# Two small reads of the weight matrices ahead of their rows, and an x tile on another queue

## The chip, the cores and the metric

The kernel runs on one core of one Trainium2 chip. The time is that of one execution on the device in microseconds (us), and the median of three runs of the kernel before is 178.54 us (178.52 to 178.56). The core has a matrix engine (TensorE, PE in the profile, with its weight loads as PEld), a vector engine (VectorE, DVE), an engine for functions of single elements (ScalarE, ACT), GpSimd (POOL) and SyncE (SP), which issues transfers here. 16 DMA engines move the data, whoever issues the transfer.

## The reference, cut to what matters

x has 2048 rows (tokens) of 512 elements, in bf16. The layer norm of x feeds two branches, and both are added to x: a linear recurrence over time with 512 complex states (branch A), and a gated feed-forward network with 1376 hidden columns (branch B).

```python
xn = _layernorm(x, axis=-1)
# branch A: h[t] = Lam_bar * h[t-1] + xn[t] @ B_bar ; y = 2 Re(h C^T) + xn * Dskip
# branch B:
g = _silu(xn @ w_gate)          # w_gate: 512 x 1376
u = xn @ w_up                   # w_up:   512 x 1376
y = (g * u) @ w_down            # w_down: 1376 x 512
out = x + A(xn) + B(xn)
```

## The kernel before

**Tiling.** The 2048 tokens are 16 tiles of 128 (`xall[:, n, :]`), and four tiles are a chunk of 512. The 512 input columns are four blocks of 128 (`KD = 4`, index k), which is the depth over which each matmul sums. The gate and up matrices come in as rows: row k is the block of 128 matrix rows with the first 1024 of the 1376 columns (`wu01`, `wg01`, 256 KB each, `load_row`, L117); the other 352 columns of all four blocks come as one transfer for each matrix into `w_end` (L113).

**The start.** TensorE first runs nine matmuls on a constant (L675). Tokens 0 to 255 (x tiles 0 and 1) take a way of their own, so that work can begin before the layer norm is known: VectorE sums each row of x (L222), TensorE transposes the tile (L231, `raw_mm`) and spreads the negative mean (L243, `mean_mm`), ScalarE copies the transposed tile out (L240, `raw_copy`), and VectorE adds the mean to it (L248, `centered`; six pieces, in the order tile 0 block 0, tile 0 block 1, tile 1 block 0, tile 1 block 1, then the last two blocks of tile 0 and of tile 1). Then TensorE multiplies these tokens by up row 0, 1, 2, 3 (L494, `row_mm(0, k)`: two tiles by two column groups, four matmuls for each row), and after that by gate row 0 to 3, with the transposed parameters (L278) and tile 2 (L231) in between. The factor 1/sigma of the layer norm comes in later, when ScalarE copies the sums out (L514, L502). VectorE meanwhile forms the statistics (L182, L183), GpSimd the inverse root (L192), and VectorE the normalised tiles (L200).

**What follows.** SyncE transposes the four normalised tiles by DMA (L258) and then the two parts of the matrix B (`BT`, L145). TensorE does the rest of chunk 0's gate and up (L494, L774), and then for each chunk the projection by B (L387, `bproj_tile`), gate and up (L462, L548), and the output by the down weights (L605) and by the matrix C folded with the parameters (L618, with `CF` from L373). VectorE carries the recurrence (L429) with its rotations (L397 to L411). Its operations are put between TensorE's by a fixed plan of costs (`pump`), at build time; each engine then works through its own list in order.

**Queues.** SyncE issues, in this order: x tile 0 (L123), up rows 0 to 3, gate rows 0 and 1, x tile 2 (L131), gate row 2, x tile 3 (L133), gate row 3, the two ends of the weights, x tiles 4 to 7 (L141), the transposes of x (L258), those of B (L145). ScalarE's queue carries x tile 1 (L125) behind a memset of VectorE (L124) that writes two elements of that tile, so that the transfer waits for it; then ScalarE loads its table of functions (L126). GpSimd's queue carries three parameter rows of 1 KB (L140).

The transfers of SyncE and ScalarE tell of their landing by eight semaphores that are handed out in turn, and a transfer is issued only when the one that had its semaphore before has landed. So x tile 2 waits for x tile 0, gate row 2 for x tile 1, x tile 3 for up row 0, gate row 3 for up row 1, the two ends for up rows 2 and 3, and x tiles 4 to 7 for gate row 0.

Of the kernel before, what the change touches and what calls it, by code (L numbers as in the profile page):

```python
# [11 lines left out]
BF16 = mybir.dt.bfloat16  # L12
# [11 lines left out]
def kernel(  # L24
# [17 lines left out]
    nc = tc.nc  # L42
# [21 lines left out]
    const = ctx.enter_context(tc.tile_pool(name="const", bufs=1))  # L64
# [15 lines left out]
    x_v = A_x[0].rearrange("(n p) d -> p n d", p=128)  # L80
# [5 lines left out]
    xall = const.tile([128, NT, D], BF16, name="xall")  # L86
# [33 lines left out]
    ident = const.tile([128, 128], BF16, name="ident")  # L120
    make_identity(nc, ident[:])
    minus_mean = const.tile([128, 128], BF16, name="minus_mean")
    nc.sync.dma_start(out=xall[:, 0, :], in_=x_v[:, 0, :])  # L123
    nc.vector.memset(xall[:, 1, 0:2], 0.0)  # L124
    nc.scalar.dma_start(out=xall[:, 1, :], in_=x_v[:, 1, :])  # L125
    nc.scalar.preload_act_table_set("silu_and_others")  # L126
    for k in range(KD):
        load_row(nc.sync, wu01, wu_v, k)
# [779 lines left out]
```

## Time and profile before

| | us |
|---|---|
| median of three runs | 178.54 |
| the profiled execution | 178.45 |
| its span, from the first to the last instruction | 176.2 |
| TensorE busy | 171.9 |
| VectorE busy | 157.6 |
| ScalarE busy | 102.7 |
| GpSimd busy | 28.1 |

The span is what the profile covers; the time of the execution has some work around it. Each line of a timeline gives the start in us, the time that it covers, engine, line of the program, operation, what is written from what, shape and count, and in brackets how long the engine was idle before it and what ended that. A queue's own instructions, which issue transfers, have a q behind the engine's name. For the transfers the profile gives the size and the time from issue to landing. In a table by stretches each engine has its busy time and the number of its instructions, and behind them stand the clock that TensorE was granted (1.00 is full), the mean busy share of the 16 DMA engines and what they moved in GB/s.

### The profile page before, as it was taken

Reading aid. Unit: us, or ns where it says so; the run is one execution under the profiler, and the core shown is the slowest. Engines: PE = TensorE matmul, PEld = TensorE weight load, DVE = VectorE, ACT = ScalarE, POOL = GpSimd, SP = SyncE. Lnnn points to the kernel's source line nnn. Section 1 sums busy time; section 2 is a strip of 40 time slices with the busy share of each in tenths; the row PEclk is TensorE's granted clock in tenths of the full one; section 3 lists DMA queues with packets and bytes.
Section 4 is the critical chain, followed back from the end, with each engine's and each line's share of the span. In section 5 each row is a group of like instructions: output and inputs, shape, how many; then the busy total and the mean of one; then the engine's idle time right before and its main releaser. Section 6 shows DMA issues by size and latency. Waiting matters only on the chain.

```text
span 176.2 us, 2377 instructions
## 1 busy us (share of the span) xinstructions
PE 171.9 (98%) x859; PEld 81.9 (46%) x859; DVE 157.6 (89%) x261; ACT 102.7 (58%) x188; POOL 28.1 (16%) x39
## 2 busy tenths in 40 slices
PE   7899999999999999999999999999999999999993
PEld 4344445464444444446444444446444444444543
DVE  3877999999999999999999999999999998699542
ACT  4179599794996685236598661024666653991100
POOL 5244110022000000044300000024100000521700
PEclk9999999999999999999999999999999999999999
DMA  5997949999999300037016000007310000696831
GB/s 169 357 342 147 142 90 208 287 188 297 151 221 309 119 0 4 0 34 85 2 30 123 0 0 0 0 0 80 43 20 12 0 0 4 93 159 106 91 87 60
DMA packets 34042, 17.87 MB, mean 101 GB/s; under 512 B 24896, under 2 KB 32928, under 8 KB 33984
## 3 DMA queue, kind: packets, MB, share of 16 engines
q1 hardware_dynamic: 30288, 14.22, 34.5%
q0 software_dynamic: 3456, 3.28, 14.6%
q10 hardware_dynamic: 288, 0.23, 0.4%
q8 instruction: 6, 0.10, 0.2%
q14 instruction: 4, 0.03, 0.1%
HBM read 8.03 MB, written 5.24 MB: 75 GB/s over the span
## 4 chain that ended last, share of the span: by engine, by line
PE 95%; DMA 3%; SPq 0%; DVE 0%; issue 0%
PE ps L462 29%; PE ps L605 22%; PE ps L618 16%; PE ps L387 16%; PE ps L494 7%; PE ps L548 3%; DMA wu<-in_B_w_up_dram 3%; PE ps L774 2%; SPq L117 0%; SPq L123 0%; DVE xall L621 0%; PE ps L231 0%; PE ps L278 0%
## 5 line engine op out<-in xcount | busy, mean ns | idle before, releaser
L605 PE MATMUL ps<-wd_sb,guT 128*128 128x512 bf16 (+4 forms) x187 | 38.9, 366 | 0.0
L429 DVE TENSOR_TENSOR_SCAN g<-r_t,car,u 128x512 bf16<-128x512 f32 x24 | 29.1, 1265 | 0.0
L618 PE MATMUL ps<-CF,wt 128*128 128x512 bf16 (+2 forms) x136 | 28.5, 366 | 0.0
L387 PE MATMUL ps<-xnT,BT 128*128 128x512 bf16 x128 | 28.3, 379 | 0.0
L605 PEld LDWEIGHTS <-guT 128*128 128x128 bf16 (+1 forms) x187 | 17.9, 98 | 20.5
L462 PE MATMUL ps<-xnT,wu 128*128 128x512 bf16 x96 | 24.6, 379 | 0.0
L462 PE MATMUL ps<-xnT,wg 128*128 128x512 bf16 x96 | 24.6, 379 | 0.0
L625 POOL DMA_DIRECT2D out_dram<-res x12 | 10.5, 1043 | 78.5 <-ACT res L624 72.5
L476 ACT ACTIVATE guT<-ps 128x512 bf16<-128x512 f32 x30 | 18.2, 606 | 4.9 <-PE ps L462 4.5
L477 ACT CAST u<-ps 128x512 bf16<-128x512 f32 x30 | 17.9, 595 | 4.8 <-PE ps L462 4.7
L389 ACT CAST u<-ps 128x512 bf16<-128x512 f32 x32 | 17.6, 594 | 4.9 <-PE ps L387 3.6
L618 PEld LDWEIGHTS <-wt 128*128 128x128 bf16 x136 | 13.0, 98 | 14.7
L387 PEld LDWEIGHTS <-BT 128*128 128x128 bf16 x128 | 12.5, 98 | 14.9
L624 ACT CAST res<-ps 128x512 bf16<-128x512 f32 x12 | 6.8, 585 | 21.4 <-PE ps L618 21.4
L579 ACT ACTIVATE xr<-xall,nb,rstd 128x512 bf16<-128x512 bf16 x16 | 11.8, 807 | 8.7 <-DVE xall L587 4.7
L462 PEld LDWEIGHTS <-wu 128*128 128x128 bf16 x96 | 9.4, 98 | 11.3
L462 PEld LDWEIGHTS <-wg 128*128 128x128 bf16 x96 | 9.3, 98 | 10.6
L192 POOL TENSOR_TENSOR rstd<-ve,neg_half 128x1 f32<-128x1 f32 (+1 forms) x7 | 7.5, 1077 | 29.4 <-DVE ve L191 28.9
L182 DVE BATCH_NORM_STATS2 stats<-xall 128x6 f32<-128x512 bf16 x16 | 10.8, 676 | 0.2 <-DMA xall<-in_A_x_dram 0.2
L462 PE MATMUL ps<-xnT,w_end 128*128 128x512 bf16 x48 | 10.8, 379 | 0.0
L481 DVE TENSOR_TENSOR guT<-guT,u 128x1024 bf16<-128x1024 bf16 x15 | 10.1, 676 | 0.0
L397 DVE TENSOR_TENSOR pm<-g,c 128x2048 bf16<-128x2048 bf16 x8 | 9.8, 1222 | 0.1
(121 smaller groups left out, 207.5 us busy)
## 6 DMA issues: line engine op xcount, KB each, us to landing
out_dram<-in_A_x_dram SPq DMA_DIRECT2D x3, 512.0 KB, 5.3
out_dram<-res POOLq DMA_DIRECT2D x12, 128.0 KB, 3.2
out_dram<-xall POOLq DMA_DIRECT2D x3, 512.0 KB, 6.7
wd_sb<-in_B_w_down_dram SPq DMA_DIRECT2D x1, 1280.0 KB, 7.9
wu<-in_B_w_up_dram SPq DMA_DIRECT2D x4, 256.0 KB, 4.6
wg<-in_B_w_gate_dram SPq DMA_DIRECT2D x4, 256.0 KB, 5.1
xall<-in_A_x_dram SPq DMA_DIRECT2D x1, 1024.0 KB, 6.9
xall<-in_A_x_dram SPq DMA_DIRECT2D x1, 512.0 KB, 6.2
```

The costliest lines, as they stand in the source:

```text
L182: nc.vector.bn_stats(out=stats[:, n, 0, :], in_=xall[:, n, :])
L387: nc.tensor.matmul(ps[:] if c else by_k(ps[:]), lhsT=BT[:, part, k, q * 128:(q + 1) * 128], rhs=xnT[:, c, k, :] if c else xnT0[:, k], star ...
L389: nc.scalar.copy(out=u_tiles[c][:, part, q, :], in_=ps[:])
L429: V.tensor_tensor_scan(out=g()[:, part, q, :], data0=r_t[:, q:q + 1].to_broadcast([128, CW]), data1=u_tiles[c][:, part, q, :], initial=ini ...
L462: nc.tensor.matmul(ps[:fs, lo:hi], lhsT=wslice(groups, fi, k), rhs=xnT[:, c, k, lo:hi], start=(k == 0), stop=(k == KD - 1))
L476: nc.scalar.activation(out=guT[:fs, fi, :], in_=psg[:fs], func=ACT.Silu)
L477: nc.scalar.copy(out=u_pair[c][:fs, fi % 2, :], in_=psu[:fs])
L494: nc.tensor.matmul(ps[:, 0:(b - a) * 128], lhsT=tokens(i, k), rhs=groups[gi][:, k, 0:(b - a) * 128], start=(k == 0), stop=(k == KD - 1))
L579: nc.scalar.activation(out=box["xr"][:], in_=xall[:, n, :], func=ACT.Identity, scale=rstd[:, n:n + 1], bias=nb[:, n:n + 1])
L605: nc.tensor.matmul(o[:], lhsT=gu_tiles[c][:fsz[fi], fi, i * 128:(i + 1) * 128], rhs=wd_sb[:fsz[fi], fi, lo:hi], start=(fi == 0), stop=False)
L618: nc.tensor.matmul(o[:], lhsT=w_tiles[c][:, part, q, i * 128:(i + 1) * 128], rhs=CF[:, part, q, lo:hi], start=False, stop=(part == 1 and q ...
L625: nc.gpsimd.dma_start(out=out_v[:, n, lo:hi], in_=res[:, lo:hi], accum_op=ALU.add)
```

## The change

A new tile `early` takes two elements (4 bytes) of each of 32 matrix rows, every 16th one, of the up matrix and then of the gate matrix. Nothing reads it. The two transfers are the first on ScalarE's queue. x tile 1 goes to SyncE's queue, between x tile 0 and the up rows, and the memset is left out.

```diff
+    early = const.tile([32, 2, 2], BF16, name="early")
     nc.sync.dma_start(out=xall[:, 0, :], in_=x_v[:, 0, :])
-    nc.vector.memset(xall[:, 1, 0:2], 0.0)
-    nc.scalar.dma_start(out=xall[:, 1, :], in_=x_v[:, 1, :])
+    for i, v in enumerate((B_w_up, B_w_gate)):
+        nc.scalar.dma_start(out=early[:, i, :], in_=v.rearrange("(r s) f -> r s f", r=32)[:, 0, 0:2])
+    nc.sync.dma_start(out=xall[:, 1, :], in_=x_v[:, 1, :])
     nc.scalar.preload_act_table_set("silu_and_others")
     for k in range(KD):
         load_row(nc.sync, wu01, wu_v, k)
```

A matrix row has 2752 bytes, so the touched places lie 44,032 bytes apart. With one transfer more ahead of the rows, the semaphores move by two places: gate row 0 is issued when x tile 0 has landed, gate row 1 after the early read of up, x tile 2 after the early read of gate, gate row 2 after x tile 1; x tile 3 waits for up row 0, gate row 3 for up row 1, and the others as before. No other instruction is added, removed or put in another order on any engine.

## The prediction

> **What bounds the kernel now.** I read the chain of waits first, then the first 23 us engine by engine, because the chain says that nothing after them matters by itself.
>
> ```profile
> span 176.2 us, 2377 instructions
> PE 95%; DMA 3%; SPq 0%; DVE 0%; issue 0%
> 1.65 4.53 DMA wu<-in_B_w_up_dram
> 6.18 0.04 issue
> 6.22 3.61 PE ps L494 x16
> ```
>
> The profiled execution took 178.45 us for a span of 176.2, so 2.25 lie around the span; the median of the runs shown is 178.54, 0.09 above it. TensorE is the chain from 6.22 on, back to back to the end. What stands ahead of it is one transfer: the second row of the up weights, issued at 1.65 and landed at 6.18. So the time can fall only if TensorE begins its unbroken run earlier, and only as far as nothing later makes it wait. The timeline of TensorE and VectorE shows the start closely:
>
> ```profile
> 3.13 0.42 DVE L222 SCALAR_TENSOR_TENSOR xnT<-xall 128x256 bf16<-128x256 bf16 x1 [1.59 <-DMA xall<-in_A_x_dram]
> 3.50 0.43 DVE L222 SCALAR_TENSOR_TENSOR xnT<-xall 128x256 bf16<-128x256 bf16 x1
> 4.01 1.67 DVE L248 TENSOR_TENSOR CF<-xnT,ps 128x128 bf16<-128x128 bf16 x6
> 4.88 0.33 PEld L494 LDWEIGHTS <-CF 128*128 128x128 bf16 x3 [0.41 <-DVE CF L248]
> 6.22 2.75 PE L494 MATMUL ps<-wu,CF 128*128 128x512 bf16 x12 [0.73 <-DMA wu<-in_B_w_up_dram]
> 8.81 0.38 PE L494 MATMUL ps<-wg,CF 128*128 128x512 bf16 x1
> ```
>
> The twelve matmuls of rows 1 to 3 run from 6.22 to 8.81, 0.216 each. Their tokens were ready long before: six centering pieces in 1.67 from 4.01 are 0.28 each, so the four that row 1 needs were there at 4.01 + 4 x 0.28 = 5.13. Row 0's last two matmuls began at 4.88 and gave way at 4.88 + 2 x 0.216 = 5.31. Without the wait for row 1, TensorE goes on at 5.31 instead of 6.22: 0.91 us are there to be had.
>
> Why row 1 is late is in the transfers, grouped by stretches (columns: PE, PEld, DVE, ACT, POOL busy, granted clock, DMA share, GB/s), and in the issues with size and time to landing:
>
> ```profile
> 3.50:4.50 1.00, 0.89 (x10) 0.59 (x8) 0.93 (x6) 0.92 (x4) 0.04 (x1) 1.00 0.85 261
> 4.50:5.50 1.00, 0.99 (x4) 0.21 (x3) 0.96 (x4) 0.28 (x2) 0.00 (x0) 1.00 0.93 298
> 6.50:7.50 1.00, 1.00 (x6) 0.42 (x5) 0.93 (x4) 0.00 (x0) 0.58 (x1) 1.00 1.03 374
> 7.50:8.50 1.00, 1.00 (x6) 0.49 (x5) 0.51 (x4) 0.07 (x1) 0.66 (x1) 1.00 1.05 391
> 39.50:41.00 1.50, 1.50 (x9) 0.69 (x7) 1.43 (x5) 1.11 (x4) 1.35 (x2) 1.00 0.91 185
> 42.50:44.00 1.50, 1.50 (x9) 0.69 (x7) 1.50 (x4) 0.19 (x1) 0.00 (x0) 1.00 1.08 371
> wu<-in_B_w_up_dram SPq DMA_DIRECT2D x1, 256.0 KB, 2.9
> ```
>
> From 3.5 to 5.5, when up rows are read for the first time, the engines of the DMA are 0.89 busy and move 280 GB/s, which is 314 for a full share; from 6.5 to 8.5 they move 382 at 1.04, 368 for a full share. Busy but moving less means packets that stand still. The first touch of the down weights shows it again: 185 / 0.91 = 203 for a full share in its first 1.5 us, 371 / 1.08 = 344 three microseconds later. A transfer is landed when its slowest engine is done, so a few stalled packets cost row 1 far more than the mean. Row 0 landed at 1.19 + 2.9 = 4.09; at 368 GB/s the next 256 KB need 0.71, so row 1 would be there at about 4.8 without stalls, ahead of 5.31.
>
> **The change part by part.** *Gone:* the memset of VectorE and ScalarE's wait for it, 0.06 us ahead of an engine that waits for x until 3.13 anyway: nothing. *Moved:* x tile 1.
>
> ```profile
> 0.74 0.39 SPq L123 DMA_DIRECT2D xall<-in_A_x_dram  x1
> 0.90 0.37 ACTq L125 DMA_DIRECT2D xall<-in_A_x_dram  x1
> 1.19 1.84 SPq L117 DMA_DIRECT2D wu<-in_B_w_up_dram  x4
> 1.31 1.28 ACT L126 ACT_TABLE_LOAD   x1 [1.31 <-DVE e_t L162]
> 3.58 1.20 ACT L240 CAST xnT<-ps 128x256 bf16<-128x256 f32 x4 [0.99 <-PE ps L231]
> xall<-in_A_x_dram SPq DMA_DIRECT2D x1, 128.0 KB, 2.4
> xall<-in_A_x_dram ACTq DMA_DIRECT2D x1, 128.0 KB, 2.5
> prm_rows<-in_A_Lambda_re_dram POOLq DMA_DIRECT2D x1, 1.0 KB, 4.0
> ```
>
> Its issue goes from 0.90 on ScalarE to 1.19 on SyncE, and every row behind it is issued 0.43 later (0.74 to 1.19 is one issue). Landing: at best as fast as tile 0, 1.19 + 2.4 = 3.6; at worst like the transfer that stands second on that queue now, 1.19 + 2.9 = 4.1. Its sum started at 3.50, when VectorE came free, so the centering chain slips by 0.1 to 0.6; I take 0.2, nearer to tile 0, which has the same size. The later issue of the rows costs nothing: row 1 is issued at 1.65 and the DMA comes to it only after row 0, landed at 4.09; 0.43 lies inside that queue time. If the queue were empty, it would be the whole 0.43.
>
> *Added:* two issues on ScalarE ahead of the table load. At 0.37 to 0.43 each from 0.74 on, the load starts at 1.6 and ends at 2.9; ScalarE's first copy is at 3.58, so it is covered with 0.7 to spare. New waits stand on SyncE's queue, since landing semaphores are handed out in turn: the first gate row waits for x tile 0, the second for the early up transfer, x tile 2 for the early gate transfer, the next for x tile 1. SyncE comes to them at about 3.5, 3.9 and 4.4. An early transfer lands like x tile 1 (0.74 + 2.5 = 3.2) or, if it meets stalls, like the 1 KB parameter row (4.0 after issue: 4.7 to 5.2). Gate rows and everything behind on that queue would be held up to 0.8 then, with rows 1 to 3 of up still to be moved: covered.
>
> *What the touches do to the DMA:* the trace has no row for a 4-byte read. Bounds for the delay of x and thereby of the chain: 0, if the touches run beside tile 0, when the engines are not full; and 1.4, row 1's own lateness (6.18 - 4.8), which is that of the slowest engine. Between them stands the first touch of the down weights, 203 instead of 344 for a full share over 1.5 us, 0.41 x 1.5 = 0.6 us lost per engine on average. I take 0.1, near the lower end, because the touches come while the DMA has little else to do. With the 0.2 above the centering chain slips by s = 0.3.
>
> Here a rule speaks against the change. The 1 KB parameter row needed 4.0 us where 128 KB of x needed 2.5: a small transfer lands with the stalls of its neighbours. The Trainium skill, "DMA: Bandwidth & Descriptors", section "Queues, rings and completion order", says that an engine's semaphore increment lands only after every earlier write of that engine, across its queues; by that rule a stalled touch holds back x although x stands on another queue. The parameter row agrees; whether touches stall, no row shows. By it s would be at its upper end and the time that of the second rival.
>
> *What takes over.* If row 1 comes in time, TensorE gains 0.91 - s. The next thing it waits for is the transposed B matrix:
>
> ```profile
> 8.48 0.41 DVE L200 TENSOR_SCALAR CF<-xall,mv,rstd 128x512 bf16<-128x512 bf16 x1 [0.46 <-POOL rstd L192]
> 9.14 0.69 DVE L182 BATCH_NORM_STATS2 stats<-xall 128x6 f32<-128x512 bf16 x1 [0.24 <-DMA xall<-in_A_x_dram]
> 12.17 0.73 DVE L200 TENSOR_SCALAR CF<-xall,mv,rstd 128x512 bf16<-128x512 bf16 x2 [0.59 <-POOL rstd L192]
> 12.61 2.69 SPq L258 DMA_TRANSPOSE xnT<-CF  x2
> 15.35 3.92 SPq L145 DMA_TRANSPOSE BT<-in_A_B_re_dram  x1
> BT<-in_A_B_re_dram SPq DMA_TRANSPOSE x1, 6.8
> 22.69 6.79 PEld L387 LDWEIGHTS <-BT 128*128 128x128 bf16 x32
> 67.34 5.38 DVE L373 SCALAR_TENSOR_TENSOR CF<-CT,nc2im,cm 128x512 bf16<-128x512 bf16 x8
> 73.04 5.13 PE L618 MATMUL ps<-CF,wt 128*128 128x512 bf16 x23
> ```
>
> B lands at 15.35 + 6.8 = 22.15 and is loaded at 22.69: 0.54 to spare. Its issue follows, on SyncE, the transposes of x, which follow VectorE's normalising at 12.17, and that chain goes back through 9.14 and 8.48 to the centering. In it stands one wait for a transfer, 0.24 for x tile 2, which goes if the slow engines are no longer late; then B moves by s - 0.24. So B allows TensorE to be early by 0.54 + 0.24 - s = 0.78 - s. That is below 0.91 - s and decides. Further on, the four C pieces that the first output needs are ready at 67.34 + 7 x 0.67 = 72.0 for matmuls up to 73.04 + 3 x 0.216 = 73.7: 1.6 to spare, no bound.
>
> The sum: 178.45 - (0.78 - 0.3) = 177.97 for an execution like the profiled one, and 0.09 more for the median: 178.06, rounded to **178.1**.
>
> **The rivals.** *The stalls stay.* They may belong to each DMA engine by itself, or to something else at that time, such as the parameter transfers of GpSimd. For it: the gate rows, first touched after 6.5, run at 368 without a slow start, so first touch alone isn't the rule. Against it: the slow start of the down weights. Then row 1 lands at 6.18 as before, or up to 0.43 later by the issue: 178.54 to 178.97, likeliest 178.6. x late by 0.3 would not show, since tokens are ready 0.9 ahead.
>
> *The stalls move in front of x (slower).* The touches stall on the same 16 engines, ahead of x tile 1 and of the rows; place: VectorE's second sum at 3.50, and all that follows to B. Price: s. From s = 0.78 on the kernel is slower than before; with the touches at 1.0 (midway between 0.6 and 1.4) and 0.2 of x tile 1's move s is 1.2 and the time 178.54 + 1.2 - 0.78 = 178.96; at both upper ends, 1.4 + 0.6, it is 179.76. For it: 64 touches on 16 engines are four each, one behind the other, and the lateness of the parameter row. Against it: the first quarter of up rows landed in 2.9 in spite of first touch.
>
> *Half way:* the stalls go, but s lies between 0.42 and 0.78, and the gain is under 0.36: 178.2 to 178.55.
>
> **How the numbers follow.** 0.2% of 178.54 is 0.36 us, about what a measurement of this kernel can tell from no change; so the bounds are 178.18 and 178.90. Forecast 0.47 (177.75 to 178.18, from s = 0 to 0.42); half way 0.10; stalls stay 0.20, of which 0.15 within the bounds and 0.05 above; stalls in front of x 0.23. Faster 0.47, within 0.25, slower 0.28. The range for 8 of 10 goes from the lower end, s = 0, 177.76 rounded to 177.7, up to 179.1, into the slower rival; the forecast's own is 177.75 to 178.2.
>
> **What would show it.** Right: the idle time of TensorE ahead of row 1's matmuls is below 0.2, the DMA's rate for a full share from 3.5 to 5.5 is near 368, the matmuls of the gate start at about 8.2 instead of 8.81, and a short wait for B stands at about 22.2. x tile 1's sum starts at 3.7. Wrong: row 1 is still awaited after 6.1 (the stalls stayed), or the second sum starts after 4.3 (they moved in front of x). A gain above 0.8 would mean that B isn't bound to VectorE's chain.

## The result and the profile after

| | before | after |
|---|---|---|
| median of 22 executions each, taken together (us) | 178.51 | 178.94 |
| their range | 178.1 to 179.29 | 178.44 to 181.0 |
| the profiled execution | 178.45 | 180.63 |
| its span | 176.2 | 178.6 |
| first matmul of the gate | 8.81 | 10.87 |
| from the end of the last matmul to the end of the span | 2.71 | 3.08 |

The kernel became slower: ratio 1.0043, interval 1.0024 to 1.0062. The mean rose by 0.77, more than the median, because the executions spread: six of the 22 took 179.98 to 181.0 (mean 180.51), the other sixteen have a mean of 178.80, which is 0.30 above the mean of before, 178.50. The profiled execution is one of the six. One of them, 180.54, has a span of only 177.0; its excess lies outside the span, as with one execution of before (179.7 with a span of 176.4). So two things are to be explained, 0.3 us in most executions, and nearly 2 us in about a quarter of them.

The page's head and the shares of the chain after:

```profile
span 178.6 us, 2377 instructions
PE 95%; DMA 1%; DVE 1%; SPq 0%; issue 0%; DVEq 0%
```

The chain of waits after (start, duration, what):

```profile
1.19 2.36 DMA xall<-in_A_x_dram
...
4.47 0.83 DVE CF L250 x3
5.32 6.58 PE ps L496 x20
```

TensorE is again the chain to the end, and the transfer ahead of it is shorter. But the work takes longer in it: 20 matmuls in 6.58, where before's chain had 16 in 3.61 and four more add 0.86. The timeline after:

```profile
0.74 0.41 ACTq L126 DMA_DIRECT2D early<-in_B_w_up_dram  x1
1.65 1.86 SPq L117 DMA_DIRECT2D wu<-in_B_w_up_dram  x4
2.94 0.42 DVE L224 SCALAR_TENSOR_TENSOR xnT<-xall 128x256 bf16<-128x256 bf16 x1 [1.40 <-DMA xall<-in_A_x_dram]
3.58 0.43 DVE L224 SCALAR_TENSOR_TENSOR xnT<-xall 128x256 bf16<-128x256 bf16 x1 [0.20 <-DMA xall<-in_A_x_dram]
5.32 5.71 PE L496 MATMUL ps<-wu,CF 128*128 128x512 bf16 x16 [0.96 <-DVE CF L250]
10.87 0.81 PE L496 MATMUL ps<-wg,CF 128*128 128x512 bf16 x3
```

And the end of the start, where B is loaded, from the timeline further on:

```profile
24.75 1.18 PEld L389 LDWEIGHTS <-BT 128*128 128x128 bf16 x6
```

B is loaded 24.75 - 22.69 = 2.06 later than before, and the gate begins 10.87 - 8.81 = 2.06 later; the last matmul, too, ends 2.06 later. So this part of the loss happened ahead of the gate, and TensorE's plan behind it runs as before. But the span is 2.43 longer. The other 0.37 lies behind the last matmul. SyncE issues the last output, whose landing takes 1.4 in both kernels, and then comes to its first drain, behind which the program ends by the same steps in both. Each line of the second kind gives the count of an instruction, its shortest, median and longest duration in ns, and the start of its first and last. Before:

```profile
173.86 0.33 SPq L622 DMA_DIRECT2D out_dram<-xall  x1
L903 SPq DRAIN  x3: 7/7/7, 175.4 to 175.7; - x3
```

After:

```profile
175.92 0.33 SPq L624 DMA_DIRECT2D out_dram<-xall  x1
L905 SPq DRAIN  x3: 7/7/7, 177.8 to 178.1; - x3
```

From the issue to the first drain it is 1.52 before and 1.89 after (the lines round the drain to a tenth). Between them, by the trace's records, SyncE waits for semaphores in nine steps of a fixed order, 0.06 apart where nothing is awaited. Before, the last output has a semaphore of the ninth step, and the other eight steps are over when it lands. The change has two transfers more, so the handing out is shifted, the last output has a semaphore of the third step, and six steps of 0.062 follow its landing: 0.37. In all ten traces with touches, wherever they stand, the time from the last matmul to the end of the span is 3.08 to 3.10, and in eight of the nine without them 2.70 to 2.72. The ninth, which moves the parameter rows to another queue, has the last output's semaphore in the fourth step and 3.03. So the 0.30 of the ordinary executions needs no loss at the start: this end alone covers it.

The idle time of 0.96 ahead of row 0 is put down to VectorE's centering, but the first piece, all that row 0's first matmul needs, was done at about 4.2 (pieces of 0.2 to 0.28 from 3.93). The transfers tell what it was: each line has the size and the time from issue to landing, of the transfers issued around 1.65.

```profile
wu<-in_B_w_up_dram SPq DMA_DIRECT2D x1, 256.0 KB, 3.6
xall<-in_A_x_dram SPq DMA_DIRECT2D x1, 128.0 KB, 2.4
early<-in_B_w_gate_dram ACTq DMA_DIRECT2D x1, 0.1 KB, 2.3
```

Row 0 landed at 1.65 + 3.6 = 5.25, against 4.09 before. Here the releaser that is named was done long ago, and the wait was one for a transfer.

The matmuls themselves are the second thing. Their shortest, median and longest duration in ns, from the view of line 496:

```profile
L496 PE MATMUL ps<-wu,CF x24: 379/380/635, 5.3 to 17.8; 128*128 128x512 bf16 x24
```

Before, none took more than 390. In this execution the first ten of the 16 start 0.43 apart and take about 635, the last six start 0.216 apart. Ten times 0.213 is 2.1, the whole difference at the gate: at 0.216 each the 16 would have ended at 5.32 + 3.46 = 8.78, and the gate would have begun as it did before. The stretches (columns as in the prediction):

```profile
2.50:3.50 1.00, 1.00 (x11) 0.87 (x9) 0.44 (x2) 0.51 (x2) 1.00 (x2) 1.00 0.91 187
3.50:4.50 1.00, 0.86 (x8) 0.58 (x7) 0.86 (x5) 1.00 (x4) 0.04 (x1) 1.00 0.93 248
4.50:5.50 1.00, 0.18 (x1) 0.10 (x1) 1.00 (x4) 0.18 (x1) 0.00 (x0) 1.00 0.98 313
6.50:7.50 1.00, 1.00 (x4) 0.40 (x3) 0.93 (x4) 0.00 (x0) 0.58 (x1) 1.00 0.97 339
```

Two readings. From 6.5 to 7.5 TensorE is full with 4 matmuls, where before had 6, and the column of the granted clock stands at 1.00 all the same; the half rate is seen in the durations only. And from 2.5 to 3.5 the DMA moves 187 GB/s at a share of 0.91, which is 205 for a full share, where before, in the same stretch, it moved 368:

```profile
2.50:3.50 1.00, 1.00 (x10) 0.75 (x8) 0.37 (x2) 0.09 (x1) 1.00 (x2) 1.00 1.08 368
```

From 3.5 to 5.5 the stalls are still there after the change: 280 GB/s at a mean share of 0.955, 294 for a full share, where before had 314.

### The profile page after: what moved, and what is told of

Same layout as the page of the kernel before. It is cut to its first block, busy times and chain, and to the rows that moved or that the text cites. A ratio compares the mean times of both kernels' runs of the same rounds, so it can differ in the third digit from the quotient of the medians.

```text
span 178.6 us, 2377 instructions
## 1 busy us (share of the span) xinstructions
PE 173.8 (97%) x859; PEld 82.6 (46%) x859; DVE 157.7 (88%) x260; ACT 104.1 (58%) x188; POOL 28.1 (16%) x39
## 4 chain that ended last, share of the span: by engine, by line
PE 95%; DMA 1%; DVE 1%; SPq 0%; issue 0%; DVEq 0%
PE ps L464 29%; PE ps L607 21%; PE ps L620 15%; PE ps L389 15%; PE ps L496 9%; PE ps L550 3%; PE ps L776 2%; DMA xall<-in_A_x_dram 1%; DVE CF L250 1%; SPq L124 0%; DVE xall L623 0%; DVE xnT L224 0%; PE ps L233 0%; PE ps L280 0%; DVEq L250 0%
```

## The experiments

All ratios are to the kernel before, run beside on the same chip; 'mean above' is the difference of the mean times. Two theories stood at first: the later issue of the rows is the loss (*issue*), or the touches are (*touches*); the clock came as a third.

### Each half alone

*x tile 1 to SyncE's queue, no touches:*

```diff
-    nc.vector.memset(xall[:, 1, 0:2], 0.0)
-    nc.scalar.dma_start(out=xall[:, 1, :], in_=x_v[:, 1, :])
+    nc.sync.dma_start(out=xall[:, 1, :], in_=x_v[:, 1, :])
```

> x tile 1 second on SyncE's queue, without the two touches. If the later issue of the up rows (0.46) is what makes row 0 late, most of the 0.43 us stays: ratio to before about 1.002 to 1.004, and executions above 179.2 us appear as with the full change. If the touches are the cause, the ratio is 1.000 within 0.001 and row 0 lands at about 4.5 at the latest. In the profile: where row 0's matmuls start up to 0.5 us later than 4.36 and run at 0.43 each, the clock is part of the cost.

*The touches alone, behind x tile 1 on ScalarE's queue, so that nothing else moves:*

```diff
     nc.scalar.dma_start(out=xall[:, 1, :], in_=x_v[:, 1, :])
+    early = const.tile([32, 2, 2], BF16, name="early")
+    for i, v in enumerate((B_w_up, B_w_gate)):
+        nc.scalar.dma_start(out=early[:, i, :], in_=v.rearrange("(r s) f -> r s f", r=32)[:, 0, 0:2])
```

> The kernel before with the two touches behind x tile 1 on ScalarE's queue; x and the rows are issued as before. If the touches take the stalls out of the rows, row 1 lands before 5.5 instead of 6.18, the rate for a full share of the DMA from 3.5 to 5.5 is near 368 GB/s and the ratio is below 0.999. If touches warm nothing and cost little, ratio 1.000 within 0.001. If touches make stalls, ratio above 1.002.

Measured: the move alone 178.69 against 178.38, 1.0005 (0.9974 to 1.0035), mean 0.30 above, one execution of 12 at 180.43; the touches alone 178.45, 1.0004 (0.9979 to 1.0028), mean 0.04 above. Neither interval excludes no change, nor, for the touches, the 0.37 at the end. The traces say more. The chain of waits with the move alone:

```profile
2.60 4.99 DMA wu<-in_B_w_up_dram
7.63 2.75 PE ps L493 x12
```

and row 0 there, from issue to landing:

```profile
wu<-in_B_w_up_dram SPq DMA_DIRECT2D x1, 256.0 KB, 2.9
```

Row 0 needs 2.9 as before, from an issue 0.46 later: it landed 0.46 later, one for one. Yet the wait in the chain is not for it, and not for row 1 any more, but for row 2, issued at 2.60 and landed at 7.59: the wait has changed its row. The touches alone, standing where they take no place from the rows, left everything as it was; their chain:

```profile
1.65 4.65 DMA wu<-in_B_w_up_dram
6.34 3.61 PE ps L497 x16
```

Row 1 is awaited to 6.30, as without touches (6.18). They made nothing faster. In this profile the gate begins at 8.93 and the last matmul ends 0.12 later than before, but the span is 0.51 longer: the other 0.39 is the end.

The move alone and the whole change were run again side by side, to see the two apart:

> x tile 1 on SyncE without touches, timed again beside the full change on the same chip. If the place in the issue order is the whole cause, it equals the full change within 0.1% (both 1.002 to 1.006 to before, first gate matmul above 9.2). If the touches carry the loss, it stays at 1.000 to 1.001 while the full change is at 1.004.

> The full change again, as the measure for the run before: ratio 1.002 to 1.006, about a quarter of its executions above 179.8.

Measured: the move alone 178.35 against 178.14, 1.0014 (0.9992 to 1.0037), mean 0.29 above, one of 12 at 180.3; the whole change 178.67, 1.0030 (1.0011 to 1.0050), mean 0.53 above. The touches in front add some 0.24 to the move in the mean, which the intervals do not separate; the end, 2.71 in the profile of the move and 3.10 in that of the whole change, is of this size. Without its one long execution the move alone is 0.13 above before in this set and, both sides without theirs, 0.20 in the first. In the chain of the whole change, this time without the half rate, the same row 2 stands:

```profile
2.60 4.29 DMA wu<-in_B_w_up_dram
6.89 0.04 issue
6.93 2.75 PE ps L496 x12
```

This gives a sum that fits the traces in which the half rate doesn't hold TensorE up: the gate begins at the latest of the four rows' landings, each with 0.04 and the matmuls that are left from that row on, 0.216 each. Here 6.93 + 8 x 0.216 = 8.66 (seen: 8.65); with the move alone at first 7.63 + 1.73 = 9.36 (seen: 9.36; five matmuls run at half rate there, but are over when row 2 lands); before, from row 1, 6.22 + 12 x 0.216 = 8.81. Row 0 may be late by more than a us without deciding; row 2 has 8 matmuls behind it and may not. What a place costs row 0 is therefore not what it costs the kernel.

### What a place in the order of issue costs

*Both touches on SyncE's queue between x tile 0 and the rows; x tile 1 stays on ScalarE's. The rows are issued two places, 0.92, later:*

```diff
     nc.scalar.dma_start(out=xall[:, 1, :], in_=x_v[:, 1, :])
+    early = const.tile([32, 2, 2], BF16, name="early")
+    for i, v in enumerate((B_w_up, B_w_gate)):
+        nc.sync.dma_start(out=early[:, i, :], in_=v.rearrange("(r s) f -> r s f", r=32)[:, 0, 0:2])
```

> The kernel before with both touches on SyncE's queue, between x tile 0 and the up rows; x tile 1 stays on ScalarE's queue. Every row is issued two places, 0.9 us, later, and nothing else changes. If the place in the issue order sets when the rows land, row 0 lands at 4.9 to 5.1 instead of 4.1 and the first gate matmul starts at 9.5 to 9.9 instead of 8.8: ratio 1.004 to 1.006. If the DMA's backlog hides the issue, as the prediction had it, ratio 1.000 to 1.001 and row 1 at 6.2 as before.

Measured: 179.75 against 178.32, 1.0075 (1.0048 to 1.0102). Of its seven executions three took 178.56 to 178.85 and four 179.75 to 179.99; the profile is of one of the first kind. The stretch and row 0 there:

```profile
2.50:3.50 1.00, 1.00 (x11) 0.82 (x10) 0.54 (x3) 0.16 (x2) 1.00 (x2) 1.00 0.60 106
```

```profile
wu<-in_B_w_up_dram SPq DMA_DIRECT2D x1, 256.0 KB, 2.7
```

Two places more leave the DMA 0.60 busy at 106 GB/s, so there was no backlog in which the later issue could hide. Row 0 landed at 4.85, 0.79 later than before, close to what the expectation has for it. But the gate began at 8.86, not at 9.5 to 9.9: rows 1 and 2 landed at 5.65 and 7.09 (before: 6.18 and 6.72), and row 2 decided. The span is 0.45 longer, of which 0.05 stands ahead of the gate and 0.39 at the end. So row 0's landing went with its place, and the gate's begin did not. The mean is 1.0 above before; the 0.39 of the end are in it, and the rest comes from the four longer executions.

> The kernel with both touches on SyncE's queue once more. Its profile before this was one of its short executions (178.61), with row 0's matmul at 4.89 and no row matmul at 0.43. If it is a long one this time (179.75 to 179.99), the clock theory wants five or more row matmuls at 0.43 and the first gate matmul at 9.8 to 10.2.

This execution took 179.08. Row 0 landed at 5.35, the gate began at 8.92, close to the 8.86 above, and the span, 177.0, is 0.3 longer: the transposed B landed at 22.96 and was loaded at 23.00, so here B held TensorE up. The kind that takes 179.8 was not caught in a profile, and its cause stays open.

*Row 1 on ScalarE's queue, behind x tile 1, so that SyncE issues rows 2 and 3 earlier:*

```diff
     nc.scalar.dma_start(out=xall[:, 1, :], in_=x_v[:, 1, :])
+    load_row(nc.scalar, wu01, wu_v, 1)
...
-    for k in range(KD):
+    for k in (0, 2, 3):
         load_row(nc.sync, wu01, wu_v, k)
```

> The kernel before with up row 1 issued on ScalarE's queue behind x tile 1 (at 1.3 instead of 1.65), which puts up rows 2 and 3 and all gate rows 0.45 earlier on SyncE's. If the issue order sets the landings, rows 2 and 3 land 0.3 to 0.5 earlier, the first gate matmul starts at 8.2 to 8.5 and the ratio is 0.997 to 0.999, held by the wait for B. If stalls alone set them, first gate matmul at 8.8 and ratio 1.000.

Measured: 178.39, 1.0011 (0.9993 to 1.0029): nothing gained. TensorE there:

```profile
4.73 4.60 PE L495 MATMUL ps<-wu,CF 128*128 128x512 bf16 x16 [0.49 <-DMA wu<-in_B_w_up_dram]
```

Row 0 landed at 4.69, 0.6 later than before although it was issued as before: with row 1 issued 0.35 earlier beside it, the row that is needed first came later. Rows 2 and 3 did land 0.5 earlier (6.21 and 6.91 for 6.72 and 7.38), as expected. But the first five of the 16 matmuls run at half rate, a thing that the next part but one takes up, and the gate began at 9.17 instead of 8.2 to 8.5. By the sum above, with row 1 landed at 5.97, it would have begun at 8.60 at the full rate. So this trace does not show that the order itself gains nothing.

*The touches first on ScalarE's queue and x tile 1 behind them, third; SyncE's order as before:*

```diff
-    nc.vector.memset(xall[:, 1, 0:2], 0.0)
+    early = const.tile([32, 2, 2], BF16, name="early")
+    for i, v in enumerate((B_w_up, B_w_gate)):
+        nc.scalar.dma_start(out=early[:, i, :], in_=v.rearrange("(r s) f -> r s f", r=32)[:, 0, 0:2])
     nc.scalar.dma_start(out=xall[:, 1, :], in_=x_v[:, 1, :])
```

> The touches stay first on ScalarE's queue, and x tile 1 goes back there as the third transfer; the rows are issued from 1.19 as before. If only the place in SyncE's order counts, row 0 lands at 4.0 to 4.2, and the ratio is 0.999 to 1.001. If the touches ahead of the rows cost something by themselves (row 0 landed 0.3 later with them than without in the profiles of the changed order), row 0 lands at 4.3 to 4.5 and the ratio is 1.001 to 1.003. In both, x tile 1 lands about 0.6 later than before, which the tokens' 0.9 to spare cover.

*Both x tiles on ScalarE's queue, so that the rows are first on SyncE's:*

```diff
-    nc.sync.dma_start(out=xall[:, 0, :], in_=x_v[:, 0, :])
-    nc.vector.memset(xall[:, 1, 0:2], 0.0)
+    nc.scalar.dma_start(out=xall[:, 0, :], in_=x_v[:, 0, :])
     nc.scalar.dma_start(out=xall[:, 1, :], in_=x_v[:, 1, :])
```

> Both x tiles go to ScalarE's queue, without the memset, and nothing stands ahead of the up rows on SyncE's: row 0 is issued at 0.74 instead of 1.19. Theory (a row lands by its place in SyncE's order of issue): row 0 lands about 0.45 earlier than before's 4.06, at 3.6 to 3.8, and the matmuls of the gate begin at 8.3 to 8.6 instead of 8.81; ratio 0.997 to 0.999, unless x tile 1, now second on ScalarE's queue, is late by more than 0.7, since the centered tokens are then awaited instead. Rival (the rows wait behind a backlog in the DMA, so that their place in the issue costs nothing): row 0 lands at 4.0 to 4.2 as before, ratio 1.000.

Both ratios were missed by far: 181.23 and 180.64 against 178.17, ratios 1.0156 (1.0116 to 1.0197) and 1.0137 (1.0109 to 1.0164). With the touches ahead of x tile 1, the transfers issued from 1.15 to 1.75 (row 0 took 3.25 and row 1 3.72, and the line has the median) and the timeline:

```profile
wu<-in_B_w_up_dram SPq DMA_DIRECT2D x2, 256.0 KB, 3.5
xall<-in_A_x_dram ACTq DMA_DIRECT2D x1, 128.0 KB, 3.9
```

```profile
5.57 0.43 DVE L224 SCALAR_TENSOR_TENSOR xnT<-xall 128x256 bf16<-128x256 bf16 x1 [2.25 <-DMA xall<-in_A_x_dram]
6.26 5.29 PE L496 MATMUL ps<-wu,CF 128*128 128x512 bf16 x16
```

Row 0 landed at 4.44, 3.25 after its issue, where the five kernels that issue row 0 at 1.19 with x tile 1 alone on ScalarE's queue ahead of it needed 2.84 to 3.04: this half of the second expectation was met. But x tile 1, issued 0.75 later than before (1.65 for 0.90), landed 2.15 later, at 5.55, just behind the two rows that were issued in the meantime. I had allowed 0.6 for it. It also stands behind the two touches on its own queue, the second of which landed only at 3.99; whether the rows or the touches held it back, this run does not separate. The second sum starts at 5.57 instead of 3.50, the tokens' 0.9 to spare are gone, and after the idle time eight of the 16 matmuls run at half rate. With the rows first, the same from the other side:

```profile
4.14 0.42 DVE L221 SCALAR_TENSOR_TENSOR xnT<-xall 128x256 bf16<-128x256 bf16 x1 [2.61 <-DMA xall<-in_A_x_dram]
...
5.07 0.42 DVE L221 SCALAR_TENSOR_TENSOR xnT<-xall 128x256 bf16<-128x256 bf16 x1 [0.49 <-DMA xall<-in_A_x_dram]
...
5.76 4.58 PE L493 MATMUL ps<-wu,CF 128*128 128x512 bf16 x16
```

Row 0, issued 0.45 earlier, landed at 3.93, only 0.13 earlier, and the sums of the two x tiles start 1.0 and 1.6 later. Here x has no touches ahead of it, so the rows beside it are what made it late. Five of the 16 matmuls run at half rate in this profile, too. With the rows behind both x tiles row 0 loses 0.46; with x beside the rows x loses 1.0 to 1.6, and the kernel loses more than by the change. None of the orders tried beat that of before, with the x tiles on two queues and the rows behind one of them.

The Trainium skill, "DMA: Bandwidth & Descriptors", section "Issuing engines are not separate DMA queues", says that issuing on several engines only saves the time of the sequencer that starts a transfer, which it calls usually small beside the transfer. The traces agree with the first half; here that time, 0.46 for one place, was the whole of row 0's delay.

### Where the stalls belong

*The gate rows loaded in the place of the up rows (and the up rows in theirs), the computation's order unchanged:*

```diff
     for k in range(KD):
-        load_row(nc.sync, wu01, wu_v, k)
+        load_row(nc.sync, wg01, wg_v, k)
     for k in range(HK):
-        load_row(nc.sync, wg01, wg_v, k)
+        load_row(nc.sync, wu01, wu_v, k)
```

(and likewise for the two that follow)

> The kernel before with gate rows loaded where up rows are loaded and the other way round; TensorE still needs up rows first, so it starts some 3 us late. If the slow start belongs to the up matrix (first touch, and gate for some reason not), gate rows run at 350 GB/s or more for a full share of the DMA from 3.5 to 5.5 and up rows are slow from 6.5 to 8.5. If it belongs to the time after the start, gate rows are slow from 3.5 to 5.5 (300 to 330) and up rows fast after 6.5.

Measured, one execution: 183.69, as TensorE waits for the up rows. The stretches:

```profile
3.50:4.50 1.00, 0.86 (x8) 0.66 (x7) 0.90 (x5) 0.99 (x4) 0.05 (x1) 1.00 1.02 284
4.50:5.50 1.00, 0.00 (x0) 0.00 (x0) 1.00 (x4) 0.23 (x1) 0.00 (x0) 1.00 0.92 288
...
6.50:7.50 1.00, 0.00 (x0) 0.00 (x0) 0.93 (x4) 0.00 (x0) 0.58 (x1) 1.00 1.01 363
7.50:8.50 1.00, 0.12 (x1) 0.10 (x1) 0.54 (x3) 0.00 (x0) 0.66 (x1) 1.00 1.07 398
```

Now the gate rows are slow from 3.5 to 5.5 (278 and 313 for a full share) and the up rows, first read after 6.5, are fast (359 and 372). The stalls belong to the start of the loads and not to one matrix or its first touch, so touches of the matrices had nothing to take away. The slow start of the down weights, which had spoken for the first touch, no run here explains.

*No transfers on GpSimd's queue; the three parameter rows go to SyncE's, ahead of the last gate row:*

```diff
+    for i, v in enumerate((A_Lambda_re, A_Lambda_im, A_log_dt)):
+        nc.sync.dma_start(out=prm_rows[i * NQ:(i + 1) * NQ, :], in_=v.rearrange("(q j) -> q j", j=128))
...
-        nc.gpsimd.dma_start(out=prm_rows[i * NQ:(i + 1) * NQ, :], in_=v.rearrange("(q j) -> q j", j=128))
```

> The kernel before with the three parameter rows of 1 KB issued on SyncE's queue ahead of gate row 3 instead of on GpSimd's. If GpSimd's transfers make the stalls of the up rows, the rate for a full share from 3.5 to 5.5 is near 368 and row 1 lands before 5.5, the first gate matmul starts at about 8. If not, row 1 lands at 6 to 6.3 as before. The parameters land at about 10 to 11 instead of 8.1, so TensorE waits for them by up to 2 us ahead of gate row 1: the ratio tells nothing, the landings do.

Measured: 179.30 against 178.32, 1.0066 (1.0045 to 1.0088); the parameters come late there, which its time contains, and so is 0.32 of the end. The landings of rows 1 to 3, by which this was to be told, are not in the trace; what is left is the rate. The stretch in question:

```profile
3.50:4.50 1.00, 1.00 (x10) 0.69 (x9) 0.97 (x6) 0.89 (x4) 0.00 (x0) 1.00 1.03 248
```

At a share of 1.03 it moves 248, 241 for a full share: the slow stretch is there without GpSimd's transfers, if shorter, as the next microsecond has 364 for a full share. What makes it is not settled by these runs.

### TensorE's clock

*Before without its nine matmuls on a constant:*

```diff
-    dummy(warm, 4, CW)
-    dummy(warm, 5, 128)
```

> The kernel before without the nine matmuls on a constant at its start; transfers, their order and all other work are unchanged, nothing of the result is left out. If TensorE's clock decides how long the row matmuls take, all of them run at 0.43 instead of 0.216 for some microseconds, the first gate matmul starts at 10 to 11 instead of 8.8 and every execution takes 179.5 to 180.8: ratio 1.007 to 1.012. If the landing of the rows decides, ratio 1.000 to 1.002.

Measured: 178.82 against 178.25, 1.0030 (1.0007 to 1.0052). TensorE there:

```profile
4.35 5.89 PE L494 MATMUL ps<-wu,CF 128*128 128x512 bf16 x16
10.08 1.03 PE L494 MATMUL ps<-wg,CF 128*128 128x512 bf16 x4
```

With the transfers as before (row 0 landed at 4.07, row 1 at 6.10), ten of the 16 matmuls run at half rate and the gate begins 1.27 later. So the half rate alone, without any change of transfers, can have a price of this size. This is one of the two longest of the eight executions (179.48; they took 178.28 to 179.58), so not every one paid it, and the ratio of 1.007 to 1.012 was missed. The Trainium skill, "TensorE: Matmul & The Clock Gate", section "Part 1: The HAM clock gate (the 'warmup' mystery)", says that the array runs at half its clock until it has been busy for a window of about 3.4 us, and that the window runs freely, so that the point differs from run to run. The starts 0.43 and 0.216 apart agree; the length of the window no run here measures.

*The whole change, twice more, one execution each:*

> The changed kernel once more, one look. If the long executions (179.9 to 181.0) are those in which the clock stays at half during the row matmuls, this one, if it takes 178.4 to 179.3, has at most five row matmuls at 0.43 and its first gate matmul at 8.8 to 9.5; if it takes above 179.9, ten or more. If something else makes them long, two executions that differ by over 1 us have the same count.

> As for the run before this one: the time above 178.4 goes with the count of row matmuls at 0.43.

Measured: 179.84 and 180.45. The first has no half rate, but a late row 2:

```profile
4.75 1.89 PE L496 MATMUL ps<-wu,CF 128*128 128x512 bf16 x8 [0.61 <-DVE CF L250]
8.20 1.02 PE L496 MATMUL ps<-wu,CF 128*128 128x512 bf16 x4 [1.57 <-DMA wu<-in_B_w_up_dram]
```

The second has the half rate again, ten matmuls, and no late row:

```profile
4.92 5.86 PE L496 MATMUL ps<-wu,CF 128*128 128x512 bf16 x16
```

So the long executions have two causes, and the one does not need the other. Among these three kernels and before they go with x tile 1 on SyncE's queue: with 0.38 taken off where there are touches, spans of 177.5 or more are five of 34 with the change (two sets) and three of 24 with the move alone, against none of 12 with the touches alone and one of 127 of the kernel before. Why the move brings them is not shown.

*Matmuls on a constant in TensorE's idle time ahead of row 0: eight with the change, eight with before, and 17 with the change (five of them ahead of tile 1's transposes):*

```diff
+    dummy(warm, 8, 128)
     for k in range(KD):
         row_mm(0, k)
```

> The changed kernel with eight more matmuls of 128 columns on the constant ahead of row 0's matmuls (0.44 us of TensorE at full clock, 0.86 at half). If the time lost is TensorE's clock, which stays at half because TensorE idles ahead of row 0, the row matmuls run at 0.216 each, the median falls to 178.4 to 178.6 and executions above 179.5 us disappear. If the late row 0 alone costs, the median stays at 178.9 or rises by up to 0.4, and the slow executions stay.

> The kernel before with the same eight matmuls. By the clock theory they cost nothing, as row 1 is awaited for 0.9 us later on, and take the slow executions (up to 179.3) away: median 178.3 to 178.5. If TensorE's time ahead of row 0 counts in full, the median rises to 178.9.

> The changed kernel with 17 more matmuls of 128 columns on the constant: 5 while TensorE waits for x tile 1, 12 ahead of row 0 (0.65 us at full clock, 1.3 at half). If idle time ahead of row 0 keeps TensorE at half clock, no execution is above 179.8 now and the ratio falls to 1.001 to 1.003. If late rows make the long executions, they stay at a quarter and the ratio at 1.004 or more.

Measured: with the change and eight 178.93, 1.0043 (1.0010 to 1.0076), two of 12 at 180.9; before with eight 178.40, 1.0000 (0.9984 to 1.0017); with 17 178.98, 1.0045 (1.0028 to 1.0062), none of 12 above 179.58. Filling the idle time lowered neither the mean nor the median. In the profile with 17 nothing runs at half rate:

```profile
4.99 1.89 PE L496 MATMUL ps<-wu,CF 128*128 128x512 bf16 x8
7.20 1.89 PE L496 MATMUL ps<-wu,CF 128*128 128x512 bf16 x8 [0.32 <-DMA wu<-in_B_w_up_dram]
```

and row 2 decides once more: 7.20 + 8 x 0.216 = 8.93. That is 0.12 behind before; the rest of the 0.49 by which the span is longer is the end. Since the whole change without filling had no execution above 179.21 in the same set of runs either, it stays open whether the filling takes the long executions away.

## Why the prediction was wrong

It said 178.1, faster; it is 178.94, slower.

**The step that failed first** is the one on which the gain stood, that the touches take the stalls out of the up rows. They were read as belonging to the first touch of a matrix, and row 1 was to land at about 4.8. The rival "the stalls stay" named the evidence against this, the fast start of the gate rows; loading the gate rows first shows it outright, and with the touches alone row 1 landed at 6.30, no earlier than the 6.18 of before, and no gain in time is seen. With that the 0.91 were not to be had this way. Why the loads start slowly stays open.

**A term was missing at the end.** That the semaphores move by two places was known, and its effect was followed only on SyncE's issues at the start. At the end it costs 0.37 to 0.39 in every trace with touches, for the prediction nothing. The sixteen ordinary executions are 0.30 longer than before in the mean. So the end covers all of it, and in these executions no loss at the start is left to explain. The timing of the touches alone, 0.04 above before with an interval up to 0.5, neither shows the end's price nor excludes it; the traces show it.

**The later issue of the rows** "costs nothing: row 1 is issued at 1.65 and the DMA comes to it only after row 0". This was half right. It does not hold for row 0's landing, which has only x ahead of it: it paid 0.46 one for one (the 0.43 of the text is 0.45 by its own rows, 0.74 to 1.19). But row 0 doesn't decide. With the move alone the ordinary executions are 0.13 and 0.20 longer in the mean, which the intervals do not tell from nothing, and with two places more the profiled gate began 0.05 and 0.11 later.

**The wait did not go but changed its row.** "Without the wait for row 1, TensorE goes on at 5.31" took rows 2 and 3 as in time. Row 1 did land earlier with the change (by 6.0 in all traces of it, instead of 6.18), and so it did with the move alone (5.25 and 5.56), without touches. But row 2 then landed at 6.89 to 8.16 instead of 6.72. By the sum above, with the full rate and the landings of six traces with the change (two of them with matmuls added), the gate would begin at 8.65, 8.81, 8.82, 8.93, 9.46 and 9.93, against before's 8.81. The last is that of the execution that took 179.84. None comes near the 8.2 that the prediction gave as its sign.

**Another term was missing:** TensorE's clock. The prediction took 0.216 for every matmul. With half the rate on ten of them the profiled execution lost 2.06. The excess of the six long executions over the sixteen, (180.51 - 178.80) x 6 / 22, is the other 0.47 of the mean's 0.77. One of the six has its excess outside the span; how much of the rest is the clock and how much late rows, two causes seen once or twice each, is not settled.

**What held:** x tile 1's landing (3.6 predicted, 1.19 + 2.4 = 3.59 by the row) and the table load behind the two issues (from 1.66 to 2.94, ahead of ScalarE's first copy at 3.43). The slip s was below 0.1 by the second sum in the profiled execution (3.58 for 3.50) instead of 0.3, though 0.7 in the execution of 180.45, where x tile 1 landed at 4.21. The small transfers landed in 2.0 and 2.3, so that SyncE's new waits held nothing up. B's cap was not put to the test by the change itself; where the gate began early, with the move alone at 8.32, B landed at 22.21 and was loaded at 22.25, and there was nothing to spare, as predicted for a gain of about half a us.

**Of the rivals,** "the stalls stay" had the right mechanism, and 178.94 lies in its 178.54 to 178.97. That it lies near the upper end is luck: the price there is "up to 0.43 later by the issue", and what the traces show instead is the end of the program, 0.37, which no rival had. It also had the wrong row. "The stalls move in front of x" did not decide: the small transfers landed in 2.0 and 2.3, and where x tile 1 was late by 0.7 in one execution, the half rate set the gate's begin.

## What to carry to other kernels

Ahead of the first work, ask of each transfer what the DMA moves in the microsecond after it: if it has no backlog there, one more place in the order of issue can delay the next transfer's landing by a whole issue. When a wait for one piece is to go, work out for each later piece when it is due (its landing and the work still behind it), since the next late one takes its place. TensorE's first matmuls may run at half rate: read the durations of single matmuls, not only their sum or the clock column. And compare the kernels at several marks, the first gate matmul, the last matmul and the end of the span: two transfers that nobody waits for cost 0.37 behind the last matmul.

## What the runs showed of the hardware

The DMA has a slow stretch at the start of the loads, whatever it reads. In every kernel at least one of the three microseconds from 3.5 to 6.5 had 215 to 312 GB/s for a full share, where from 7.5 to 8.5 all had 359 to 375. It isn't tied to one moment: it stood at 3.5 to 4.5 without GpSimd's transfers (241), and at 5.5 to 6.5 with the rows issued two places later (237 and 245 in two executions). Reads of 4 bytes from 32 places each took 1.8 to 2.8 us to land where they were issued ahead of the rows, 3.0 and 4.1 where they stood behind x tile 1, and no later read is seen to gain by them. At the end of the program SyncE's waits for the landing semaphores took 0.06 each, one after the other, so that it cost 0.37 which of them the last output had. The half rate of the matmuls (0.43 between starts, about 634 ns each) ended at different times in executions of the same kernel, from ahead of row 0 to about 9.5 us, with the granted clock at 1.00 in the page throughout.
